# Order of the first K projection, shared input channels, LN2 on ScalarE and the order of group 1's stores in a pre-LN attention and MLP kernel

## The chip, the cores and the metric

The kernel runs on one core of a Trainium2 chip. The metric is the device time in microseconds of one execution, as a median of several runs. The engines are TensorE (PE in the profile, its weight loads PEld), VectorE (DVE), ScalarE (ACT), GpSimd (POOL) and SyncE (SP), which here issues most of the DMAs. Each engine takes its instructions in the order in which the program writes them.

## The reference

One transformer block over 2048 tokens of 576 channels, in bfloat16: local attention with 32 heads of 18 channels over 8 keys at a stride of 2, then an MLP of width 4608. A layer norm stands before the attention, and two stand one after the other before the MLP.

```python
def reference(A_x, A_wqkv, A_wo, B_x, B_w1, B_b1, B_w2, B_b2):
    def _A_ref(x, wqkv, wo):
        H = 32; Dh = D // H
        W, dil = 8, 2
        q, k, v = (x @ wqkv) in heads of Dh
        idx = pos[:, None] - (jnp.arange(W) * dil)[None, :]
        logits = jnp.einsum("bhsd,bhswd->bhsw", q, k at idx) * scale
        logits = jnp.where(idx >= 0, logits, -1e9)
        attn = _softmax(logits, axis=-1)
        o = jnp.einsum("bhsw,bhswd->bhsd", attn, v at idx)
        return o @ wo
    def _B_ref(x, w1, b1, w2, b2):
        y = _layernorm(x, axis=-1)
        h = _gelu(jnp.einsum("bsd,df->bsf", y, w1) + b1)
        return jnp.einsum("bsf,fd->bsd", h, w2) + b2
    h = x + _A_ref(_layernorm(x, axis=-1), A_wqkv, A_wo)
    return h + _B_ref(_layernorm(h, axis=-1), B_w1, B_b1, B_w2, B_b2)
```

## The kernel before

**Tiles and order.** The tokens stand in 16 tiles of 128, numbered so that a key two tokens back lies in the tile two numbers lower. The even tiles are projected first (0, 2, ... 14), then the odd ones. Attention and MLP take the tiles in groups of two, in the order 14, 12 (group 0), 10, 8 (group 1), 6, 4, 2, 0, then 15 down to 1. `A` is that order in the code, `EVEN` and `ODD` the order of projection. The order of all instructions on each engine is the order in which the program calls them; lists of calls (`after`, `between`, `hooks`, `loads`, and for the MLP `m1`, `ia`, `ib`) say what stands behind which step.

**A projection.** A contraction over 576 channels is four blocks of 128 and a rest of 64. Each matmul uses 64 rows of the array, so that two run side by side. `phase` (line 209) runs the two column halves (`g`) of an output: in the first phase half 0 takes rows 0 to 63 and half 1 rows 64 to 127 of five blocks (10 matmuls), in the second phase the rows change over for four blocks (8 matmuls). Between the two phases of one output stands a marker: `marker` (225) puts a no-operation on POOL that waits for the first phase, and the second phase waits for it. `visit` (230) runs the first phases of two or three outputs and then their second phases, each followed by its evacuation (`evac`), which is an activation on ScalarE for Q, K and V. Q, K and V take 24 visits, called 0 to 23 here, with two outputs each: visit 0 is K of tiles 0 and 2, visit 1 their V, the even tiles last until visit 11, the odd ones from 12. Visits 17 and 19 carry the output projection (`wo_duo`) of tiles 14 and 12 as a third output. PSUM has three pairs of banks in rotation for Q, K and V, and a pair "D" for other things.

**The rest of 64 channels.** For x (Q, K, V), block 4 of the transposed tile holds channels 448 to 575; half 0 uses 448 to 511 from it and takes 512 to 575 in place of them in block 3. For the attention output o, for the normalized h and for `wo` and `w1`, block 4 holds channels 512 to 575 twice, once for each half of the rows. `transpose_in` (177) makes the second copy by two more matmuls, `dma_out` (196) by a second short store into the DRAM tile `td`, from which a transposing DMA reads `oT` or `hnT`.

**Start.** Tile 0 is loaded in two halves, tile 2 in one. `ln1_first` (833) takes the mean of both tiles on ScalarE (line 840), the statistics on DVE (846, 855), and subtracts the mean on DVE (`center`, 821). `ln1_even_rstd` (857) takes the roots on POOL. `tr_x` (260) transposes both tiles on PE and copies them (267), the first on ScalarE, part of the second on DVE. Visit 0 comes after both.

**LN2 of the first two tiles.** After visit 17, `ln2` (462) adds x to the output projection of tile 14 on DVE (457) and takes statistics on DVE (148, 149, 155); behind it comes `att_qk_a` of tile 10. After visit 18 the root is taken on POOL, b2 is added into the residual (`add_b2`, 498) and a bias is made on DVE (170). Between the evacuations of visit 19, ScalarE applies the norm (174), and in visits 21 and 22 `tr_h` transposes tiles 14 and 12. Tile 12 follows two visits later in the same way. In visit 18, behind the second evacuation, stands `tr_o` of tile 12, whose copy `oT` (420) is on ScalarE. In later groups `ln2_act` (470) does the same on ScalarE: mean, square, variance (474 to 476), root on POOL (477).

**Queues.** SP's queue holds, in order, weight loads (`load`, which waits for the last evacuation), the stores and reads of K and V (`store_halo`, `halo`: a tile's ring slot is written to DRAM and read back one row lower), stores and reads of odd x (`out_x`, `in_x`: through DRAM, transposed), of o (`send_o`, `read_o`) and of normalized h, and the output stores. Wo's quarters are loaded after visits 6, 8, 11 and 12.

**Group 1 (k = 1 in the loop over groups).** In group 0's second MLP part, `read_o(e)` and an output store are issued (`ib[8]`). Group 1 begins with the weighted sum of values of tile d = 4 (`pv_sum`, with the halo load of V between its parts), its store, then QK of the next tile, the halo load of K, the read of o and seven ring stores (`halos`). The output projections of both tiles stand at the begin of its second MLP part (`ia[0]`).

Of the kernel before, what the change touches and what calls it, by code (L numbers as in the profile page):

```python
# [17 lines left out]
def kernel(  # L18
# [100 lines left out]
    def load_wo(qs):  # L119
        src = A_wo.rearrange("(h d) c -> h d c", h=H)  # L120
        for q in qs:
            load(wo_sb[q * H:(q + 1) * H, :, :], src[:, q:4 * KF:4, :])
            load(woh_sb[q * H:(q + 1) * H, :], src[:, 4 * KF + q % 2, q // 2 * HALF:(q // 2 + 1) * HALF])

    def load_w1h():
        load(b1_bf[:], B_b1.rearrange("(ft p) -> ft p", p=P))
        src = B_w1[KF * P:D, :].rearrange("p (u g c) -> p u g c", u=NU // 3, g=2)
        for r in range(2):
            load(w1h_sb[half_rows(r), :].rearrange("p (u c) -> p u c", u=NU // 3), src[:, :, r, :])

    def load_w1(c):
        cols = slice(c * F // 6, (c + 1) * F // 6)
        load(w1_sb[:, :, cols], B_w1[0:KF * P, cols].rearrange("(k p) c -> p k c", p=P))

    def load_w2(c):
        f0, f1 = (0, 4, 7, 11, 14, 21, FA, FT)[c:c + 2]
        dst = w2a_sb[:, f0:f1, :] if f1 <= FA else w2b_sb[:]
        load(dst, B_w2[f0 * P:f1 * P, :].rearrange("(ft p) c -> p ft c", p=P))
# [38 lines left out]
    def transpose_in(pair, src, twice=True):  # L177
        def turn(rows, kt, c):
            for r in range(2):
                block = src[half_rows(r), c:c + P if rows.start is None else D]  # L180
                nc.tensor.matmul(pair[rows, r, kt * HP:(kt + 1) * HP], lhsT=block, rhs=ident[half_rows(r), half_rows(r)],
                                 start=True, stop=True, skip_group_check=True)

        for kt in range(KT):
            turn(slice(None), kt, min(kt * P, D - P))
        if twice:
            turn(half_rows(0), KF, KF * P)
# [8 lines left out]
    def dma_out(src):  # L196
        td = dram.tile([P, KT * P], BF16, tag="td", name="td", bufs=4)
        nc.sync.dma_start(out=td[:, 0:D], in_=src)
        stored[0] = nc.sync.dma_start(out=td[:, D:KT * P], in_=src[:, KF * P:D]).ins
# [6 lines left out]
    def half_rows(r):  # L206
        return slice(r * HP, (r + 1) * HP)

# [21 lines left out]
    def visit(makes, hook=None, between=(), late=None):  # L230
# [6 lines left out]
        for make in makes:  # L237
# [3 lines left out]
            elif isinstance(hook, dict) and len(duos) in hook:  # L241
                hook[len(duos)]()
        for n in range(len(makes) + (late is not None)):
# [16 lines left out]
    def tr_x(j, tag):  # L260
        pair = psum_pair(tag or "CAB"[(ring_pos[0] + 1) % 3], "xt_pt")
        transpose_in(pair, q_all[:, j, :], False)
# [26 lines left out]
    def store_halo(j, ts=slice(0, 2)):  # L289
        nc.sync.dma_start(out=kv_dram[j, 1:P + 1, ts, :], in_=kv_ring[j % 2][:, j // 2, ts, :])  # L290

    def qkv_duo(j, t):
        def make():
# [3 lines left out]
            def op(g, i, sl, kt):  # L297
                c0 = g * HALF
                if g == 0 and kt == KF - 1 and sl.start:
                    kt = KF  # L300
# [126 lines left out]

    def read_o(j):
        nc.sync.dma_start_transpose(out=new_oT(j)[:], in_=o_sent.pop(j)[:])
# [3 lines left out]
    def wo_duo(j, tag):  # L433
        def make():
# [3 lines left out]
            def op(g, i, sl, kt):  # L438
                c0 = g * HALF
                return t[sl, kt, :], (wo_sb[sl, kt, c0:c0 + HALF] if kt < KF else woh_sb[sl, :])  # L440
# [29 lines left out]
    def ln2_act(j):  # L470
        h = h_of[j]
        y = sb.tile([P, D], BF16, tag="hn", name="hn", bufs=2)
        nmean, var, rstd = (sb.tile([P, 1], F32, tag=f"ln2_{t}", name=f"ln2_{t}", bufs=2) for t in ("nmean", "var", "rstd"))
        nc.scalar.activation(out=y[:], in_=h[:], func=ACT.Identity, scale=-1.0 / D, accum_out=nmean[:])
        nc.scalar.activation(out=y[:], in_=h[:], func=ACT.Square, bias=nmean[:], accum_out=var[:])
        nc.scalar.activation(out=var[:], in_=var[:], func=ACT.Identity, scale=(1.0 + EPS) / D, bias=eps2[:])
        ins = nc.gpsimd.tensor_tensor(out=rstd[:], in0=var[:], in1=mhalf[:], op=ALU.pow).ins  # L477
        root[0] = ins if j not in GROUPS[1] else None
        hn[j] = (h, rstd, nmean, y)

    def ln2_send(j):
# [3 lines left out]
        hn[j] = dma_out(y[:])  # L485
# [56 lines left out]
    def mlp1_duo(grp, us, tag):  # L542
        def make():
# [5 lines left out]
            def op(g, i, sl, kt):  # L549
                f0 = fts[g][i] * P  # L550
                c0 = (GF * us[i // GF] + i % GF) * P
                return (w1_sb[sl, kt, f0:f0 + P] if kt < KF else w1h_sb[sl, c0:c0 + P]), ht[sl, kt, 0:N]
# [225 lines left out]
    with tc.manual_schedule(engines={ENG.PE, ENG.Activation, ENG.DVE, ENG.SP, ENG.Pool}):  # L778
# [8 lines left out]
        load_wqkv(2, 0, 2)  # L787
        load_wqkv(2, 2, KF)
        load_wqkv_tail(nc.sync, 2)
        load_x(EVEN[3:4])  # L790
# [42 lines left out]
        def ln1_first():  # L833
            junk = q_all[:, ODD[-1], :]
            parts = []
            for gi in range(2):
                x = x_all[:, EVEN[gi], :]
                stats, mv, nmean = (qp.tile([P, n], F32, name=f"ln1_{gi}_{t}") for t, n in
                                    (("stats", 2 * nc.vector.BN_STATS_DIM), ("mv", nc.vector.BN_AGGR_DIM), ("nmean", 1)))
                nc.scalar.activation(out=junk, in_=x, func=ACT.Identity, scale=-1.0 / D, accum_out=nmean[:])  # L840
                parts.append((x, halves(stats[:]), mv, nmean))
                ln1[gi] = (mv[:].unsqueeze(1), None)

            def stat(gi, c):
                x, stats, _, _ = parts[gi]
                nc.vector.bn_stats(out=stats[:, c, :], in_=x[:, c * HALF:(c + 1) * HALF])

            for gi in range(2):
                stat(gi, 0)
                if gi == 0:  # L850
                    stat(gi, 1)
                center(EVEN[gi], parts[gi][3][:, 0:1], ALU.add)
                if gi == 1:
                    stat(gi, 1)
                nc.vector.bn_aggr(out=parts[gi][2][:], in_=parts[gi][1])
# [24 lines left out]
        ln1_first()  # L880

# [41 lines left out]
        for n, v in enumerate((19, 19, 20, 20, 21, 22)):  # L923
# [18 lines left out]
            17: [c_(ln2, A[0]), c_(att_qk_a, A[2])],  # L942
# [194 lines left out]
```

## Time and profile before

| what | value |
|---|---|
| median of 3 runs | 362.56 us (362.54 to 363.0) |
| the profiled execution | 366.0 us |
| its span, first to last instruction | 364.2 us |
| mean granted TensorE clock | 0.994 |
| PE busy | 355.0 us (97%), 4942 matmuls |
| DVE busy | 296.6 us (81%) |
| ACT busy | 235.3 us (65%) |
| POOL busy | 45.5 us (13%) |
| DMA | 46.29 MB, mean 127 GB/s |

The busy digits of PE and its granted clock in 40 equal slices of 9.1 us, with those of DVE between them:

```profile
PE   7999999999999799999999999999999999999996
DVE  5999999999989889994799989989998998520431
PEclk9999999999999989999999999999999999999999
```

A digit is the busy share in tenths, 9 is 90% or more; for PEclk it is the granted clock. The profile takes one execution. A wait is put down to what came last by the semaphores, so a wait for several things names one of them. Spans on POOL are rough.

### The profile page before, as it was taken

What the parts mean: (1) busy time and instruction counts of PE and PEld (TensorE: products, weight loads), DVE (VectorE), ACT (ScalarE), POOL (GpSimd) and SP (SyncE); (2) the same over time, 40 slices, a digit from 0 to 9 for tenths busy, and PEclk for the clock granted to TensorE, in tenths of its full rate; (3) what the DMA queues carried; (4) which work ended last, traced back from release to release, by engine and by line L of the source; (5) the groups of instructions that cost most, each with busy time, mean ns of one, the idle gap of its engine ahead of it and who ended that gap; (6) DMA issues with size and microseconds to landing.
All of it is one profiled execution on the core that took longest, in us unless ns stands there. A gap on an engine that the chain in (4) does not pass through costs nothing.

```text
span 364.2 us, 11562 instructions
## 1 busy us (share of the span) xinstructions
PE 355.0 (97%) x4942; PEld 292.8 (80%) x4942; DVE 296.6 (81%) x417; ACT 235.3 (65%) x521; POOL 45.5 (13%) x61
## 2 busy tenths in 40 slices
PE   7999999999999799999999999999999999999996
PEld 3778977887789777887788778877887788778874
DVE  5999999999989889994799989989998998520431
ACT  4879756897637782468846956695669566805630
POOL 2240004000112010100020102020202020210000
PEclk9999999999999989999999999999999999999999
DMA  7986799963447584651283466344545354263001
GB/s 247 329 278 191 197 218 306 373 227 72 143 90 110 174 207 71 114 90 39 74 121 81 62 133 93 90 98 122 86 88 65 93 85 58 52 120 51 4 1 32
DMA packets 62980, 46.29 MB, mean 127 GB/s; under 512 B 32192, under 2 KB 60736, under 8 KB 62928
## 3 DMA queue, kind: packets, MB, share of 16 engines
q1 hardware_dynamic: 58960, 41.50, 43.2%
q0 software_dynamic: 3744, 3.84, 9.9%
q8 instruction: 38, 0.62, 0.7%
q10 hardware_dynamic: 224, 0.22, 0.2%
q14 instruction: 14, 0.11, 0.1%
HBM read 23.38 MB, written 12.42 MB: 98 GB/s over the span
## 4 chain that ended last, share of the span: by engine, by line
PE 79%; DVE 11%; DMA 6%; ACT 2%; issue 1%; POOL 0%; ACTq 0%; SPq 0%; POOLq 0%
PE pm L216 33%; PE po L664 25%; PE po L576 9%; PE pq L216 7%; PE pw L216 4%; DVE ln_stats L148 2%; DMA x_all<-in_A_x_dram 2%; DMA oT<-td 2%; DVE prod L393 1%; DMA xnT<-xd 1%; DVE prod L399 1%; DVE prod L347 1%; ACT h_all L557 1%; DVE ln_mv L149 1%; DVE prod L338 1%
## 5 line engine op out<-in xcount | busy, mean ns | idle before, releaser
L216 PE MATMUL pm<-hnT,w_sb 64*128 64x256 bf16 x2304 | 143.0, 269 | 0.0
L557 ACT ACTIVATE h_all<-pm,b_sb 128x256 f16<-128x256 f32 (+1 forms) x288 | 108.6, 496 | 51.0 <-PE pm L216 50.4
L216 PEld LDWEIGHTS <-w_sb 64*128 64x128 bf16 x2304 | 113.5, 94 | 13.4 <-issue 1.7
L664 PEld LDWEIGHTS <-h_all 128*128 128x128 f16 x480 | 46.2, 98 | 13.7 <-issue 1.6
L216 PE MATMUL pq<-wq_sb,xnT 64*128 64x288 bf16 x720 | 54.7, 283 | 1.1 <-ACT kv_ring L306 0.4
L216 PEld LDWEIGHTS <-xnT 64*128 64x128 bf16 x864 | 44.0, 94 | 9.9 <-issue 0.8
L347 DVE TENSOR_TENSOR prod<-prod 128x2304 bf16<-128x2304 bf16 (+1 forms) x64 | 44.2, 691 | 2.0
L338 DVE TENSOR_TENSOR prod<-kv_ring,q_all 128x4608 bf16<-128x4608 bf16 x16 | 40.9, 2556 | 3.2 <-POOL ln_rstd L477 2.5
L393 DVE TENSOR_TENSOR prod<-kv_ring,probs 128x4608 bf16<-128x4608 bf16 x16 | 40.9, 2558 | 0.8 <-DMA kv_ring<-kv_dram 0.3
L216 PE MATMUL pm<-hnT,w1h_sb 64*128 64x256 bf16 x288 | 39.5, 269 | 0.0
L664 PE MATMUL po<-w2a_sb,h_all 128*128 128x288 bf16 (+1 forms) x262 | 35.8, 286 | 0.0
L576 PEld LDWEIGHTS <-h_all 128*128 128x128 bf16 x288 | 28.3, 99 | 8.7 <-issue 1.2
L399 DVE TENSOR_TENSOR prod<-prod 128x2304 bf16<-128x2304 bf16 (+1 forms) x32 | 33.9, 1058 | 1.1
L664 PEld LDWEIGHTS <-kv_ring 128*128 128x128 f16 x252 | 24.6, 98 | 6.3
L576 PE MATMUL po<-w2a_sb,h_all 128*128 128x288 bf16 x224 | 29.6, 293 | 0.0
L216 PE MATMUL pq<-wqh_sb,xnT 64*128 64x288 bf16 x144 | 27.6, 283 | 0.0
L766 POOL DMA_DIRECT2D x_all<-o_sb x12 | 10.7, 890 | 126.1 <-PE pw L216 72.2
L216 PE MATMUL pw<-wo_sb,oT 64*128 64x288 bf16 x256 | 20.1, 288 | 2.4 <-DMA oT<-td 2.3
L644 DVE TENSOR_TENSOR kv_ring<-h_all 128x1536 f16<-128x1536 f16 (+3 forms) x9 | 6.8, 760 | 16.1 <-ACT h_all L557 16.1
L664 PE MATMUL po<-w2b_sb,h_all 128*128 128x288 bf16 (+1 forms) x122 | 19.7, 286 | 0.1
L216 PEld LDWEIGHTS <-oT 64*128 64x128 bf16 x288 | 13.8, 95 | 7.0 <-DMA oT<-td 3.3
L161 POOL TENSOR_TENSOR ln_rstd<-ln_veps,mhalf 128x1 f32<-128x1 f32 (+2 forms) x14 | 13.3, 964 | 48.5 <-DVE ln_veps L155 31.7
(107 smaller groups left out, 394.9 us busy)
## 6 DMA issues: line engine op xcount, KB each, us to landing
w_sb<-in_B_w_dram SPq DMA_DIRECT2D x6, 768.0 KB, 5.8
kv_ring<-kv_dram SPq DMA_DIRECT2D x28, 144.0 KB, 2.3
kv_dram<-kv_ring SPq DMA_DIRECT2D x13, 288.0 KB, 3.9
x_all<-in_B_b_dram SPq DMA_DIRECT2D x15, 144.0 KB, 3.7
w2a_sb<-in_B_w_dram SPq DMA_DIRECT2D x2, 1008.0 KB, 7.4
td<-q_all SPq DMA_DIRECT2D x14, 144.0 KB, 1.8
td<-hn SPq DMA_DIRECT2D x14, 144.0 KB, 1.8
x_all<-h POOLq DMA_DIRECT2D x14, 144.0 KB, 4.6
```

What stands on the lines that cost most here:

```text
L148: nc.vector.bn_stats(out=stats[:, i, c, :], in_=src[:, c * HALF:(c + 1) * HALF])
L161: nc.gpsimd.tensor_tensor(out=rstd[:], in0=veps[:], in1=mhalf[:].to_broadcast([P, n]), op=ALU.pow)
L216: last = nc.tensor.matmul(duo["g"][r ^ swap][i], lhsT=lhsT, rhs=rhs, start=(swap == 0 and i == 0 and kt == 0), stop=(swap == 1 and kt == K ...
L338: ins = nc.vector.tensor_tensor(out=prod[:], in0=k_ring[j % 2], in1=q_all[:, j, :].unsqueeze(1) .to_broadcast([P, W, D]), op=ALU.mult).ins
L347: nc.vector.tensor_tensor(out=prod[:, :, o * H:o * H + n], in0=prod[:, :, a * H:a * H + n], in1=prod[:, :, c * H:c * H + n], op=ALU.add)
L393: nc.vector.tensor_tensor(out=prod[:].rearrange("p w (d h) -> p w d h", h=H), in0=v_ring[j % 2].rearrange("p w (d h) -> p w d h", h=H), in ...
L399: nc.vector.tensor_tensor(out=prod[:, 0:n, :], in0=prod[:, 0:n, :], in1=prod[:, n:2 * n, :], op=ALU.add)
L557: pace[0] = nc.scalar.activation(out=hT(grp)[:, f, 0:N], in_=ps[:, r, i * N:(i + 1) * N], func=ACT.Gelu_apprx_tanh, bias=b1_sb[:, f:f + 1] ...
L576: nc.tensor.matmul(banks[half], lhsT=hT(grp)[:, f, i * P:(i + 1) * P], rhs=w2_rows(f)[:, half * HALF:(half + 1) * HALF], start=(f == 0), s ...
L644: nc.vector.tensor_tensor(out=s_slot(t, m0, m1), in0=a, in1=b, op=alu)
L664: nc.tensor.matmul(bank, lhsT=l, rhs=r, start=start, stop=stop, skip_group_check=True)
L766: nc.gpsimd.dma_start(out=x_of(j), in_=o_of.pop(j), accum_op=ALU.add)
```

## The change

It has five parts.

1. `load_wo`, `load_w1`, `load_w1h`, `transpose_in`, `dma_out`, the operands of `wo_duo` and of `mlp1_duo`: block 4 now holds channels 448 to 575 for o, Wo, LN2 and w1 too, as it does for x. The two additional matmuls of a transpose go. The last two quarters of Wo and the sixths 0, 2 and 4 of w1 are loaded in more pieces. w2 is loaded in five pieces instead of seven.
2. Start: the first tile alone is normalized with ScalarE's mean; the second one is normalized like the later ones (`ln1_even(1)`). Its transposes stand after the first phase of the first K projection, and visit 0 runs each output's second phase and evacuation right behind its first (`apart`). The load of the fourth even tile stands before the second half of V's weights.
3. LN2 of tile 14 is on ScalarE: h on DVE and the mean on ScalarE after visit 17, square, variance and root behind the first evacuation of visit 18, the norm behind the first one of visit 19.
4. Group 1's stores: the output store of tile 14 moves from group 0's second part to group 1's last step of its first part, the halo load of V for tile d behind the store of o, and the seven ring stores wait until the read of o has landed.
5. The helper functions that these need.

```diff
     def load_wo(qs):
         src = A_wo.rearrange("(h d) c -> h d c", h=H)
         for q in qs:
-            load(wo_sb[q * H:(q + 1) * H, :, :], src[:, q:4 * KF:4, :])
-            load(woh_sb[q * H:(q + 1) * H, :], src[:, 4 * KF + q % 2, q // 2 * HALF:(q // 2 + 1) * HALF])
+            rows, k = slice(q * H, (q + 1) * H), KF - q // 2
+            load(wo_sb[rows, 0:k, :], src[:, q:4 * k:4, :])
+            if q >= 2:
+                load(wo_sb[rows, k, 0:HALF], src[:, q + 4 * k + 2, 0:HALF])
+                load(wo_sb[rows, k, HALF:D], src[:, q + 4 * k, HALF:D])
+            load(woh_sb[rows, :], src[:, 4 * KF - 2 + q, q // 2 * HALF:(q // 2 + 1) * HALF])
...
     def load_w1(c):
         cols = slice(c * F // 6, (c + 1) * F // 6)
-        load(w1_sb[:, :, cols], B_w1[0:KF * P, cols].rearrange("(k p) c -> p k c", p=P))
+        n = KF - 1 if c % 2 == 0 else KF
+        load(w1_sb[:, 0:n, cols], B_w1[0:n * P, cols].rearrange("(k p) c -> p k c", p=P))
+        for r in range(2 * (KF - n)):
+            load(w1_sb[half_rows(r), n, cols], B_w1[n * P + 2 * r * HP:n * P + 2 * r * HP + HP, cols])
 
     def load_w2(c):
-        f0, f1 = (0, 4, 7, 11, 14, 21, FA, FT)[c:c + 2]
+        f0, f1 = (0, 7, 14, 21, FA, FT)[c:c + 2]
...
-    def transpose_in(pair, src, twice=True):
...
-        if twice:
-            turn(half_rows(0), KF, KF * P)
+    def transpose_in(pair, src):
+        for kt in range(KT):
+            c = min(kt * P, D - P)
             for r in range(2):
...
     def dma_out(src):
         td = dram.tile([P, KT * P], BF16, tag="td", name="td", bufs=4)
-        nc.sync.dma_start(out=td[:, 0:D], in_=src)
-        stored[0] = nc.sync.dma_start(out=td[:, D:KT * P], in_=src[:, KF * P:D]).ins
+        nc.sync.dma_start(out=td[:, 0:KF * P], in_=src[:, 0:KF * P])
+        stored[0] = nc.sync.dma_start(out=td[:, KF * P:KT * P], in_=src[:, D - P:D]).ins
...
+    def block(g, sl, kt):
+        return KF if g == 0 and sl.start and kt == KF - 1 else kt
...
     def visit(makes, hook=None, between=(), late=None, apart=False):
...
+            if apart:
+                phase(duos[-1], 1, marks[-1])
+                duos[-1]["evac"]()
+        if apart:
+            return
...
     def read_o(j):
-        nc.sync.dma_start_transpose(out=new_oT(j)[:], in_=o_sent.pop(j)[:])
+        o_read[0] = nc.sync.dma_start_transpose(out=new_oT(j)[:], in_=o_sent.pop(j)[:]).ins
...
-                return t[sl, kt, :], (wo_sb[sl, kt, c0:c0 + HALF] if kt < KF else woh_sb[sl, :])
+                return t[sl, block(g, sl, kt), :], (wo_sb[sl, kt, c0:c0 + HALF] if kt < KF else woh_sb[sl, :])
...
     def ln2_act(j):
+        ln2_mean(j)
+        ln2_root(j)
+
+    def ln2_mean(j):
...
         nc.scalar.activation(out=y[:], in_=h[:], func=ACT.Identity, scale=-1.0 / D, accum_out=nmean[:])
+        hn[j] = (h, rstd, nmean, y, var)
+
+    def ln2_root(j):
+        h, rstd, nmean, y, var = hn[j]
         nc.scalar.activation(out=y[:], in_=h[:], func=ACT.Square, bias=nmean[:], accum_out=var[:])
         nc.scalar.activation(out=var[:], in_=var[:], func=ACT.Identity, scale=(1.0 + EPS) / D, bias=eps2[:])
         ins = nc.gpsimd.tensor_tensor(out=rstd[:], in0=var[:], in1=mhalf[:], op=ALU.pow).ins
-        root[0] = ins if j not in GROUPS[1] else None
+        root[0] = ins if j not in GROUPS[0] + GROUPS[1] else None
...
-    def ln2_send(j):
+    def ln2_norm(j):
         h, rstd, nmean, y = hn[j]
         nc.scalar.activation(out=nmean[:], in_=nmean[:], func=ACT.Identity, scale=rstd[:])
         ln_apply_act(y[:], h[:], rstd[:], nmean[:])
-        hn[j] = dma_out(y[:])
+        hn[j] = y
...
         load_wqkv(2, 0, 2)
+        load_x(EVEN[3:4])
         load_wqkv(2, 2, KF)
         load_wqkv_tail(nc.sync, 2)
-        load_x(EVEN[3:4])
...
         ln1_first()
+        ln1_even(1)
...
-        for n, v in enumerate((19, 19, 20, 20, 21, 22)):
+        for n, v in enumerate((19, 20, 21, 22)):
...
-            17: [c_(ln2, A[0]), c_(att_qk_a, A[2])],
-            18: [c_(ln2_rstd, A[0]), c_(add_b2, A[0]), c_(ln2_bias, A[0]), c_(halo, A[2], 1), c_(att_qk_add, A[2], ((0, 0, 9),))],
+            17: [c_(ln2_h, A[0]), c_(ln2_mean, A[0]), c_(att_qk_a, A[2])],
+            18: [c_(add_b2, A[0]), c_(halo, A[2], 1), c_(att_qk_add, A[2], ((0, 0, 9),))],
...
-            18: {1: [c_(tr_o, A[1], "D")]},
-            19: [c_(ln2_hn, A[0])],
+            18: {0: [c_(ln2_root, A[0])], 1: [c_(tr_o, A[1], "D")]},
+            19: [c_(ln2_norm, A[0])],
...
         hooks = {
+            0: {1: lambda: call([c_(tr_x, EVEN[1], "C"), c_(ln1_even, 2)])},
...
-        tr_x(EVEN[1], "C")
-        ln1_even(2)
...
-            visit(duos, hooks.get(qd), between.get(qd, ()))
+            visit(duos, hooks.get(qd), between.get(qd, ()), apart=qd == 0)
...
         def halos(n):
             for _ in range(min(n, len(pending_halo))):
-                store_halo(pending_halo.pop(0))
+                ins = store_halo(pending_halo.pop(0))
+                if o_read[0] is not None:
+                    tc.add_manual_dep(ins, o_read[0].name, sync_dep, reason="stores behind the read of o")
...
-                ib[8] = [c_(read_o, e), c_(out_store, g[0])]
+                ib[8] = [c_(read_o, e)]
             elif k == 1:
-                m1[0] += [c_(pv_sum, d), c_(send_o, d)]
+                m1[0] += [c_(att_pv_sum, d), c_(send_o, d), c_(halo, d, 2)]
                 m1[1] += [c_(att_qk_a, e), c_(halo, e, 1), c_(read_o, d), c_(att_qk_b, e, 0), c_(halos, 7)]
-                m1[3] += [c_(att_qk_a, f), c_(halo, f, 1), c_(att_qk_add, f, ((0, 0, 9), (0, 0, 4)))]
+                m1[3] += [c_(out_store, GROUPS[0][0]), c_(att_qk_a, f), c_(halo, f, 1), c_(att_qk_add, f, ((0, 0, 9), (0, 0, 4)))]
```

## The prediction

> **What bounds the kernel now.** I read four views, in this order. The table of waits by engine comes first, because TensorE (PE) is busy 355.0 of 364.2 us and only its idle time can be won. The lines give who waited for whom, the total, the number of waits and the longest one.
>
> ```profile
> PE pw L216 <- DMA oT<-td: 2.3, 2, 2.2
> PE xt_pt L181 <- DVE q_all L821: 1.4, 2, 1.2
> PE pq L216 <- ACT kv_ring L306: 0.4, 2, 0.2
> PE pq L216 <- POOLq L226: 0.2, 1, 0.2
> ```
>
> Two waits matter: the output projection that waits for an attention tile (2.2 us once), and the start, where the second tile's transposes wait for its centring (1.2 us). Then the timeline of PE and of SP's queue around the first (start, us, engine, line, operation, count, idle time before it):
>
> ```profile
> 124.34 0.30 PE L216 MATMUL pw<-woh_sb,oT 64*128 64x288 bf16 x2
> 126.80 0.66 PE L216 MATMUL pw<-wo_sb,oT 64*128 64x288 bf16 x8 [2.15 <-DMA oT<-td]
> 129.00 8.15 PE L576 MATMUL po<-w2a_sb,h_all 128*128 128x288 bf16 x56
> 138.95 7.02 PE L576 MATMUL po<-w2a_sb,h_all 128*128 128x288 bf16 x56
> ...
> 116.27 0.58 SPq L769 DMA_DIRECT2D out_dram<-x_all  x1
> 116.90 0.43 SPq L333 DMA_DIRECT2D kv_ring<-kv_dram  x1
> 117.87 0.45 SPq L199 DMA_DIRECT2D td<-q_all  x1
> 122.19 1.21 SPq L429 DMA_TRANSPOSE oT<-td  x1
> 123.45 4.80 SPq L290 DMA_DIRECT2D kv_dram<-kv_ring  x7
> ```
>
> The reader should see that the same 56 matmuls take 8.15 us after the wait and 7.02 us later, and that the tile's store (117.87) stands behind an output store and a halo load, while its read (122.19) shares the DMA engines with seven ring stores. The third view, stretches of one us, tells why the matmuls are slow (stretch, length, PE busy and count, granted clock, DMA share, GB/s):
>
> ```profile
> 129.00:130.00 1.00, 1.00 (x7) 0.50 1.04 396
> 132.00:133.00 1.00, 1.00 (x11) 1.00 1.06 80
> ```
>
> The granted clock is 0.50 here. The same stretches put the drop at about 127.9 to 131.3: 3.4 us at half speed, so 1.7 us lost on top of the 2.15. The fourth view is the order on the engines where LN2 moves, visits 18 and 19, with ScalarE's own price for the same work taken from group 1:
>
> ```profile
> 52.72 0.75 DVE L457 TENSOR_TENSOR h<-pw,x_all 128x576 f32<-128x576 f32 x1
> 53.16 1.19 ACT L306 ACTIVATE kv_ring<-pq 128x576 bf16<-128x576 f32 x2 [1.82 <-PE pq L216]
> 54.24 0.70 ACT L420 CAST oT<-o_pt 128x640 bf16<-128x640 f32 x1
> 56.52 0.65 ACT L306 ACTIVATE q_all<-pq 128x576 bf16<-128x576 f32 x1 [1.58 <-issue]
> ...
> 128.94 0.68 ACT L474 ACTIVATE hn<-h 128x576 bf16<-128x576 f32 x1 [2.13 <-DVE h L457]
> 129.75 0.77 ACT L475 ACTIVATE hn<-h,ln_nmean 128x576 bf16<-128x576 f32 x1
> 130.65 0.29 ACT L476 ACTIVATE ln_var<-ln_var,eps 128x1 f32<-128x1 f32 x1
> 130.85 0.67 ACT L474 ACTIVATE hn<-h 128x576 bf16<-128x576 f32 x1
> ```
>
> Start to start, the mean costs 0.81 us, the square 0.90 and the variance 0.20.
>
> **Start.** The second tile loses ScalarE's mean (5.27 to 6.05), so the first tile's copies can start at about 5.47 instead of 5.96 (transposes end 5.36, plus 0.12 as at 10.43 to 10.55). The first K projection then runs from 5.9, held by its weights (second half landed at 6.18, tail about 0.4 later) to about 6.7. DVE now takes both statistics before the second centring, which ends at about 6.68 instead of 6.45; the second transposes follow at 6.75, and its DVE copy still starts at about 7.16 (7.17 before), ScalarE's copy behind it. So the second projection starts at 7.64 as before, and only 0.24 us comes out of the visit: the eight matmuls of the first tile's second phase (8.53 to 9.02, 0.49) now lie ahead of it, but the marker between the second tile's phases has no cover any more (its first phase issues until 8.53, its last matmul ends at 8.69, POOL answers at 8.73 to 8.75), which costs 0.25. The third change is larger: tile 6's load (the fourth even tile) waits at 5.21 for a DMA slot and holds DVE for 0.62 us at 9.57. Issued at 3.97 in place of a weight half it lands near 8.25, and DVE runs 0.66 earlier; PE, which waits for centrings in visits 1 to 3, follows. I count 0 of this. At 51.23 PE already waits (0.15) for xnT, whose read is issued at 46.09 once a store has landed; the time won before ends there. Bounds: -0.7 to 0.
>
> **Shared channels.** Eight 64-column matmuls go (two in each of four transposes). Ten of them issue in 0.13 us, so 0.1 us is won. Matmul counts of projections and MLP stay. The stores of a turned tile keep their two DMAs and 160 KB. Wo's last two quarters and w1's even sixths become four and three DMAs: 4 + 6 more issues, two fewer for w2. SP issues one in 0.44 us (44.57 to 45.01). For w1 SP is idle before and after and nothing waits. For Wo, four issues (1.75 us) stand ahead of the xnT read at 46.09, two of them ahead of the halo load at 44.10. With DVE 0.66 early SP begins 0.66 sooner, so the halo load leaves at about 44.1 as before, and the xnT read at 46.4 to 46.6. Visit 18 starts 0.4 late (bounds -0.7 to +1).
>
> **LN2 on ScalarE.** DVE sheds 0.82 + 0.21 + 0.15 + 0.15 us, but its next step, adding b2, waits for b2's load (landed 57.47), so nothing is won there. ScalarE runs in order: the mean waits for h, which ends at 53.47, and behind it stand both evacuations of visit 18 and the copy of the next o. My clock for ScalarE: mean 53.5 to 54.3, evacuation to 54.9 (0.55 apart), square to 55.75, variance to 55.95, evacuation to 56.55, copy of o (0.70) to 57.2, against 54.94 before. Visit 19's output projection, which used oT at 55.16, starts at 57.25. What is left of the visit then is 34 matmuls of 0.061 (18 pairs in 1.1 us), 2.07 us, so it ends at 59.3, not 57.24. Visit 20 has 36 of them, 2.2 us, and visit 21 starts at 61.5 instead of 59.81. There part of an old wait covers the rest: its second phase stood until 61.66 for the marker behind the other tile's root, and now comes at 61.5 + 1.22 + 0.13 = 62.9. Net **+1.25 us** with visit 18's 0.4 in it. If h comes 0.66 earlier it is +0.5; if the halo load is a us late, +2.1. The root on POOL took 2.80 us beside a QK product at 54.84 and 0.56 at 131.10; at 56 DVE idles for b2, so it is short, and the markers queued behind it are not yet due.
>
> **Group 1's stores.** The output store and the halo load leave the queue ahead of the o stores: these go at about 116.3 and 116.7, 1.2 us sooner, and wait less (before, 4.3 us to land; the median of such stores is 1.8). The read follows at about 121 and, with the seven ring stores held until it has landed, should take nearer its median of 2.9 than the 4.56 of before: 124. PE comes there at 124.65 + 1.25 - 0.1 = 125.8. So the wait of 2.15 goes and the clock drop with it, 1.7. What SP holds back are the ring stores, from 123.45 to 124, and behind them output stores, b2 and LN2's store, which waits for ScalarE until 133.95 anyway. Later nothing takes it back: the transposed LN2 tiles land at 141.4 for 147.87, and DVE waits 5.00 us for PE at 169.16.
>
> The Trainium skill (TensorE: Matmul & The Clock Gate, HAM oscillation) asks for no PE gaps above some 3.4 us. By that rule a gap of 2.15 us drops no clock; the trace shows a drop after just this gap, and I follow the trace. By the rule the sum would be 1.7 us smaller.
>
> **Sum**, against the profiled execution's own 366.0 us (span 364.2): -0.1 + 1.25 - 2.15 - 1.7 = **-2.7 us**. The median of the plain runs, 362.56, lies 3.4 below the profiled one, and I can't see which idle time is shorter there. With the same change: **359.9 us**, own range 358.9 to 361.2.
>
> **Rivals.**
> 1. *The wait goes, but no clock drop is won*: it is not in the plain runs, or the 1.7 us idle in visit 19 brings another one. For it: 0.50 is granted for one 3.4 us stretch only, and 1.2 us of idle at the start brought no drop. Sum -1.0: 361.5 us.
> 2. *The read of o still comes late*, landing at 127 (issued 122.2, 4.6 us). PE then waits about 1 us and the clock may hold: -1.6, 361.0 us. Against it: two DMAs fewer ahead and no ring stores beside it.
> 3. *ScalarE's queue decides, slower*: the stall of visit 19 (1.15 net of the transposes, up to 2.0) stays, while the wait at 126.80 is an effect of the profiled execution's slower DMAs and absent in plain runs. The 3.4 us by which these are shorter is close to 2.15 + 1.7, which speaks for it; that the queue's order needs no profiler to be late speaks against. 363.7 us; it decides once the wait and its drop cost under 1.15 us in plain runs.
>
> **Chances.** Forecast 0.51, rival 1 0.22, rival 2 0.07, rival 3 0.20. A plain measurement tells 0.2% (0.73 us) from no change. The forecast gives faster nearly always, rival 1 in six of ten cases, rival 2 mostly; rival 3 slower in seven of ten, else same. Faster 0.67, same 0.16, slower 0.17. The range runs from 358.9 to 363.6, to leave out part of rival 3.
>
> **What would show it.** Right: no PE wait for oT in group 1, granted clock 1.0 through 127 to 132, the 56 matmuls at 7.0 us, and a new PE wait for ScalarE's oT or kv_ring of 1.5 to 2 us near 55 to 57. Wrong: a clock drop near 56 to 60, PE waiting over 0.5 us for oT near 126, or xnT reads that hold visit 18 by over 1 us.

## The result, and the profile after

| | before | after |
|---|---|---|
| median | 362.62 us (362.48 to 363.0) | 364.73 us (364.25 to 365.8) |
| ratio, 95% interval | 1 | 1.0065 [1.0051, 1.0078] |
| profiled execution, its span | 366.0, 364.2 us | 364.67, 362.9 us |

The change makes the kernel slower by 0.65%, some 2.4 us. The forecast was faster, 359.9 us, and its range ended at 363.6.

The profiled executions alone say the opposite: 364.67 after 366.0. So the first thing to settle is which of the two profiles is like the plain runs. The one of after is (364.67 beside a median of 364.73); the one of before lies 3.4 us above its median. Before unchanged was therefore profiled again, as the first experiment (span 361.1 us, 362.85 in all), and its lines are used below as "the second profile of before". Of the 110 plain executions of before that were recorded beside the experiments, 16 show a mean clock of 0.994 or 0.995, like the first profile (0.994): twelve of these took 361.05 to 363.85 us, as the others did (361.03 to 364.87), and four 365.7 to 368.17.

The table of waits of the kernel after answers to the first view of before (who waited for whom, total, number, longest):

```profile
PE pm L221 <- DMA hnT<-td: 1.5, 2, 1.3
PE pq L221 <- DMA xnT<-xd: 1.3, 1, 1.3
PE pw L221 <- ACT oT L429: 1.1, 1, 1.1
...
PE pw L221 <- DMA oT<-td: 0.4, 1, 0.4
```

The two waits of before, for oT's read in group 1 and for the second centring at the start, are gone. Three others are the largest now: for a transposed LN2 tile, for a transposed x tile, and for ScalarE's copy of o.

The timeline of the kernel after in group 1, TensorE first and then SP's queue (start, us, engine, line, operation, count):

```profile
123.64 2.80 PE L221 MATMUL pm<-hnT,w_sb 64*128 64x256 bf16 x48
126.27 0.67 PE L221 MATMUL pw<-wo_sb,oT 64*128 64x288 bf16 x8
...
128.58 7.03 PE L599 MATMUL po<-w2a_sb,h_all 128*128 128x288 bf16 x56
...
117.02 0.83 SPq L200 DMA_DIRECT2D td<-q_all  x1
117.89 0.45 SPq L201 DMA_DIRECT2D td<-q_all  x1
118.39 1.55 SPq L342 DMA_DIRECT2D kv_ring<-kv_dram  x2
120.92 1.24 SPq L440 DMA_TRANSPOSE oT<-td  x1
123.81 1.29 SPq L300 DMA_DIRECT2D kv_dram<-kv_ring  x3
```

Here the picture is the predicted one: the read leaves at 120.92, the ring stores stand behind it, the output projection follows without idle time, and the 56 matmuls take 7.03 us. The one-us stretches of the same place (stretch, length, PE busy, its weight loads, DVE, ACT and POOL with counts, granted clock, DMA share, GB/s) agree:

```profile
129.00:130.00 1.00, 1.00 (x11) 0.80 (x9) 0.97 (x3) 0.97 (x4) 0.00 (x0) 1.00 0.96 356
132.00:133.00 1.00, 1.00 (x10) 0.78 (x8) 0.96 (x3) 0.97 (x4) 0.00 (x0) 1.00 0.70 75
```

The clock is 1.00 in both. And yet the same output projection, used for the second tile, starts no earlier than in before: 127.37 here, 127.30 in the first profile of before, where it had waited 2.15 us. What after saves here beside the first profile, it had lost before. The timeline of visits 18 to 20 in the kernel after shows where (TensorE, then ScalarE, then DVE; in brackets the idle time before, and what ended it):

```profile
52.06 0.66 PE L221 MATMUL pq<-wq_sb,xnT 64*128 64x288 bf16 x8 [1.29 <-DMA xnT<-xd]
...
56.90 0.66 PE L221 MATMUL pw<-wo_sb,oT 64*128 64x288 bf16 x8 [1.08 <-ACT oT L429]
...
53.29 0.68 ACT L489 ACTIVATE hn<-h 128x576 bf16<-128x576 f32 x1 [2.25 <-DVE h L468]
...
53.99 0.65 ACT L315 ACTIVATE kv_ring<-pq 128x576 bf16<-128x576 f32 x1
54.54 0.77 ACT L494 ACTIVATE hn<-h,ln_nmean 128x576 bf16<-128x576 f32 x1
...
56.16 0.68 ACT L429 CAST oT<-o_pt 128x640 bf16<-128x640 f32 x1
...
58.93 0.76 DVE L522 TENSOR_TENSOR x_all<-h,x_all 128x576 bf16<-128x576 f32 x1 [3.21 <-DMA x_all<-in_B_b_dram]
...
60.87 0.75 DVE L468 TENSOR_TENSOR h<-pw,x_all 128x576 f32<-128x576 f32 x1
```

Visit 18 stands 1.29 us for the read of x, visit 19 stands 1.08 us for the copy of o behind LN2 on ScalarE, and DVE stands 3.21 us for b2. The last is the largest and the least visible (before: 0.27 us in the first profile, 0.77 in the second): DVE is not the busiest engine, but its next step, h of tile 12 at 60.87, leads into a chain of attention steps without much idle time that ends in the output projection of group 0's second tile (92.74) and, through LN2 and its transposing read, in the start of group 1's MLP (108.58, with the wait of 1.26 for hnT).

SP's queue in the kernel after says why b2 is late:

```profile
45.15 1.31 SPq L104 DMA_DIRECT2D wo_sb<-in_A_wo_dram  x3
46.52 0.41 SPq L104 DMA_DIRECT2D woh_sb<-in_A_wo_dram  x1
47.03 1.33 SPq L290 DMA_TRANSPOSE xnT<-xd  x1
48.47 0.53 SPq L286 DMA_DIRECT2D xd<-q_all  x1
...
52.76 1.85 SPq L290 DMA_TRANSPOSE xnT<-xd  x1
54.71 0.52 SPq L104 DMA_DIRECT2D x_all<-in_B_b_dram  x1
```

A quarter of Wo takes four issues instead of two, the read behind it leaves at 47.03, the store of the next odd x behind that, the read of this x waits for its store (52.76), and the load of b2 stands behind this read (54.71, landed at 58.8).

### The profile page after: what moved, and what is told of

Its sections match the earlier page's. It is cut to its first block, busy times and chain, and to the rows that moved or that the text cites. A ratio compares the mean times of both kernels' runs of the same rounds, so it can differ in the third digit from the quotient of the medians.

```text
span 362.9 us, 11553 instructions
## 1 busy us (share of the span) xinstructions
PE 353.3 (97%) x4934; PEld 295.6 (81%) x4934; DVE 295.2 (81%) x412; ACT 236.2 (65%) x525; POOL 44.1 (12%) x61
## 4 chain that ended last, share of the span: by engine, by line
PE 72%; DVE 13%; DMA 7%; ACT 3%; SPq 2%; issue 2%; POOL 0%; POOLq 0%; ACTq 0%
PE pm L221 34%; PE po L687 22%; PE pq L221 7%; PE po L599 5%; PE pw L221 4%; DVE ln_stats L155 2%; DVE prod L356 2%; DMA hnT<-td 2%; DMA x_all<-in_A_x_dram 1%; DVE prod L402 1%; DMA td<-hn 1%; DVE prod L347 1%; DVE prod L408 1%; DMA xd<-q_all 1%; ACT h_all L580 1%
## 5 line engine op out<-in xcount | busy, mean ns | idle before, releaser
L221 PEld LDWEIGHTS <-w_sb 64*128 64x128 bf16 x2304 | 115.2, 94 | 13.3 <-issue 2.9
L221 PE MATMUL pq<-wq_sb,xnT 64*128 64x288 bf16 x720 | 55.8, 288 | 2.4 <-DMA xnT<-xd 1.3
L221 PEld LDWEIGHTS <-xnT 64*128 64x128 bf16 x864 | 45.0, 95 | 11.2 <-DMA xnT<-xd 1.9
L599 PE MATMUL po<-w2a_sb,h_all 128*128 128x288 bf16 x224 | 28.5, 286 | 0.0
L496 POOL TENSOR_TENSOR ln_rstd<-ln_var,mhalf 128x1 f32<-128x1 f32 x14 | 9.8, 697 | 108.3 <-ACT ln_var L495 108.3
```

Source lines behind the costliest of these rows:

```text
L221: last = nc.tensor.matmul(duo["g"][r ^ swap][i], lhsT=lhsT, rhs=rhs, start=(swap == 0 and i == 0 and kt == 0), stop=(swap == 1 and kt == K ...
L599: nc.tensor.matmul(banks[half], lhsT=hT(grp)[:, f, i * P:(i + 1) * P], rhs=w2_rows(f)[:, half * HALF:(half + 1) * HALF], start=(f == 0), s ...
```

## The experiments

Each kernel was timed in five rounds beside before on one chip. The theory at the outset was: the wait and the clock drop of group 1 belong to one execution (rival 3's condition), and the loss comes from LN2's order on ScalarE, from the added Wo pieces in SP's queue, or from both. All ratios are to before on the same chip. The table stands in four groups of four kernels, each group on a chip of its own; the medians of before beside them are 363.03, 362.18, 361.86 and 362.93 us. So medians compare only within a group, and times from traces of different chips with a margin of about 1 us.

| kernel | median, us | ratio, 95% interval |
|---|---|---|
| before again | 363.46 | 1.0016 [0.9990, 1.0041] |
| before + channels | 366.39 | 1.0099 [1.0059, 1.0139] |
| before + LN2 | 363.79 | 1.0021 [0.9997, 1.0044] |
| before + stores | 363.45 | 1.0006 [0.9984, 1.0029] |
| before + start | 361.31 | 0.9990 [0.9970, 1.0009] |
| after, Wo's last quarters early | 366.03 | 1.0098 [1.0063, 1.0132] |
| after, LN2 on DVE | 364.76 | 1.0083 [1.0067, 1.0099] |
| after without channels | 362.41 | 1.0014 [1.0002, 1.0027] |
| after, b2 early | 363.77 | 1.0061 [1.0036, 1.0086] |
| after, Wo's quarters whole | 363.65 | 1.0055 [1.0035, 1.0075] |
| after, w1's sixths whole | 364.21 | 1.0054 [1.0035, 1.0072] |
| before + start + stores + b2 early | 361.21 | 0.9980 [0.9968, 0.9991] |
| after again | 364.34 | 1.0054 [1.0034, 1.0075] |
| after, Wo whole + b2 early | 363.32 | 1.0018 [1.0001, 1.0035] |
| the same, LN2 re-ordered | 362.36 | 1.0001 [0.9985, 1.0018] |
| without channels, b2 early, LN2 re-ordered | 361.25 | 0.9962 [0.9949, 0.9975] |

**Before again.**

> The kernel before, unchanged, for a second trace of it. If the profiled execution of before was an unusual one, this one shows a span near 360.8 us (362.6 less 1.8), no clock drop at 128 us and a wait for oT in group 1 under 0.6 us. If the wait belongs to the kernel, it shows 2 us of wait again and a span near 364. Time: same, ratio 1.000.

The waits and the timeline of this second profile of before:

```profile
PE pw L216 <- DMA oT<-td: 0.2, 1, 0.2
```

```profile
122.04 2.80 PE L216 MATMUL pm<-hnT,w_sb 64*128 64x256 bf16 x48
124.66 0.67 PE L216 MATMUL pw<-wo_sb,oT 64*128 64x288 bf16 x8
...
126.98 7.03 PE L576 MATMUL po<-w2a_sb,h_all 128*128 128x288 bf16 x56
...
58.30 0.76 DVE L499 TENSOR_TENSOR x_all<-h,x_all 128x576 bf16<-128x576 f32 x1 [0.77 <-DMA x_all<-in_B_b_dram]
...
60.31 0.75 DVE L457 TENSOR_TENSOR h<-pw,x_all 128x576 f32<-128x576 f32 x1
...
45.08 0.42 SPq L104 DMA_DIRECT2D woh_sb<-in_A_wo_dram  x1
46.15 1.32 SPq L280 DMA_TRANSPOSE xnT<-xd  x1
...
54.23 0.50 SPq L104 DMA_DIRECT2D x_all<-in_B_b_dram  x1
...
121.64 1.21 SPq L429 DMA_TRANSPOSE oT<-td  x1
122.91 5.27 SPq L290 DMA_DIRECT2D kv_dram<-kv_ring  x7
```

No wait for oT of more than 0.2 us, no pause before the 56 matmuls, and these take 7.03 us: the stall and the clock drop (3.85 us together) belong to the execution that was profiled first, not to the usual run of the kernel. The order of the queue is the same in both profiles: here, too, seven ring stores leave right behind the read of o (122.91 and 121.64). But the read lands after 2.8 us, where it took 4.6 in the first profile; why it took longer there isn't shown. Against this profile the kernel after comes 1.6 us later at the second tile's output projection (127.37 against 125.77) and at group 1's MLP (108.58 against 106.98). Of this, 0.5 us stand at the output projection of group 0's second tile already (92.74 against 92.25); most of the rest is the wait for hnT, 1.26 us against 0.15.

**The four parts alone on before**: the channels with w2's five pieces; LN2 of tile 14 on ScalarE; group 1's stores; the new order at the start with the earlier load.

> Before, with the shared channels alone (Wo and w1 in more pieces, w2 in fewer). Queue theory: SP issues four more Wo pieces ahead of the read of xnT, b2's load follows later by 1 to 1.5 us, DVE waits for b2 longer (0.3 to over 1 us) and its chain up to group 0's MLP is late by as much: slower by 1.0 to 2.0 us, 363.6 to 364.6. ScalarE theory (LN2's order is the cause): within 0.4 us of before.

> Before, with LN2 of tile 14 on ScalarE alone. ScalarE theory: PE waits 1 to 2 us for oT's copy in visit 19 and the end comes 1 to 2 us later, 363.6 to 364.6. Queue theory: PE waits there too, but DVE's chain sets group 0's MLP and doesn't move, so the wait is made up: within 0.5 us of before, 362.3 to 363.1.

> Before, with the order of group 1's stores alone. If the wait and the drop belong to before's plain runs: 2 to 3.8 us faster, 359 to 360.5. If they were in one execution only: within 0.7 us of before, 361.9 to 362.7, and no wait for oT in group 1.

> Before, with the start alone (order of the first K projection and the earlier load of the fourth even tile). Both theories: DVE's chain of the first norms runs up to 0.7 us earlier, and what PE wins is lost at the read of xnT unless SP's queue comes earlier too: 361.9 to 362.6, -0.7 to 0. If the clock is still at half speed in visit 0, up to 1 us slower.

The channels cost about 1%, more than the whole change and more than the 1 to 2 us expected. LN2 costs about 0.2%, but its interval still holds no change; the stores bring nothing that can be measured (the read of o lands after 2.8 us, as in the second profile of before), the start at most 0.3%. The timeline of before with the channels, SP's queue and then DVE:

```profile
47.77 0.41 SPq L104 DMA_DIRECT2D woh_sb<-in_A_wo_dram  x1
48.29 1.33 SPq L290 DMA_TRANSPOSE xnT<-xd  x1
...
55.93 0.52 SPq L104 DMA_DIRECT2D x_all<-in_B_b_dram  x1
...
60.06 0.76 DVE L522 TENSOR_TENSOR x_all<-h,x_all 128x576 bf16<-128x576 f32 x1 [1.94 <-DMA x_all<-in_B_b_dram]
```

The read leaves 2.14 us later than in the second profile of before (48.29 against 46.15); 0.77 of this is there before the first of these Wo loads (43.18 against 42.41), so about 1.4 is left for the four added issues. It lands 3.8 later (5.3 us after its issue, where it took 3.6; in the first profile of before, without the pieces, it took 5.1), and visit 18 starts 2.3 later (53.63 against 51.37). The addition of b2 is 1.76 us later (60.06 against 58.30), the output projection of group 0's second tile 1.88 (94.13 against 92.25), group 1's MLP 2.3 (109.29 against 106.98). The two profiled times differ by 3.2 us (366.04 and 362.85): the last 0.9 arises between 169 and 204 us, at a wait for hnT (0.36) and one for oT (0.26) among others, and was not followed further.

**Parts taken out of after.**

```diff
-        for q, v in enumerate((6, 8, 11, 12)):
-            loads[v] = [c_(load_wo, [q])]
+        for q, v in enumerate((6, 8, 4, 5)):
+            loads[v] = loads.get(v, []) + [c_(load_wo, [q])]
```

> The changed kernel, with the last two quarters of Wo (four pieces each) loaded after visits 4 and 5, when SP's queue is idle, instead of 11 and 12. Queue theory: the reads of xnT and the load of b2 come 1 to 1.5 us earlier, DVE's chain with them, and the kernel gains 1.2 to 2.4 us: 362.3 to 363.5. ScalarE theory: gains under 0.5 us, 364.2 or more.

A miss: 1.0098. The queue is no freer after visits 4 and 5. There the pieces stand ahead of the first odd x tiles' stores, whose read leaves at 34.76 instead of 30.95; visit 12 starts 2.1 us later (38.18 against 36.10), and the read at 47.03 comes later too (48.12). The block was moved, not taken away.

```diff
-            17: [c_(ln2_h, A[0]), c_(ln2_mean, A[0]), c_(att_qk_a, A[2])],
-            18: [c_(add_b2, A[0]), ...
+            17: [c_(ln2, A[0]), c_(att_qk_a, A[2])],
+            18: [c_(ln2_rstd, A[0]), c_(add_b2, A[0]), c_(ln2_bias, A[0]), ...
```

> The changed kernel with LN2 of tile 14 on DVE as before. ScalarE theory: the PE wait of 1.1 us in visit 19 goes and 1 to 2 us are won: 362.7 to 363.7. Queue theory: within 0.5 us of the changed kernel, 364.2 to 365.2, or slower still, since DVE gets 1.3 us of statistics back, partly inside its wait for b2.

Taking LN2 back brings nothing in after (1.0083, beside 1.0065 and 1.0054 for after itself). In its trace the wait for ScalarE's oT is gone, while the addition of b2 stands at 59.52 and h of tile 12 at 61.53: DVE's chain, not the stall, sets what follows. Alone on before the same stall (1.4 us) went with some 0.2%, not clear of nothing.

> The changed kernel without the shared channels (start, LN2 and stores stay). Queue theory: nothing stands ahead of xnT's read and b2's load: 362.0 to 362.9, like before or a little faster. ScalarE theory: 364 or more, since LN2's order is still there.

Without the channels 1.0014: about half a per cent comes back, with the stall of visit 19 still there (1.4 us). The add of b2 starts at 56.48 and h of tile 12 at 58.42, against 58.93 and 60.87:

```profile
56.48 0.76 DVE L520 TENSOR_TENSOR x_all<-h,x_all 128x576 bf16<-128x576 f32 x1 [1.51 <-DMA x_all<-in_B_b_dram]
...
58.42 0.75 DVE L466 TENSOR_TENSOR h<-pw,x_all 128x576 f32<-128x576 f32 x1
```

This trace is 0.76 us ahead of that of after already at the first of these Wo loads (41.20 against 41.96), so by estimate some 1.7 of the 2.45 us are the queue's. At the output projection of group 0's second tile 1.27 us are left (91.47 against 92.74), for there TensorE sets the pace: from 60 to 108 us the chain that ended last holds TensorE alone, while in after DVE's steps are the largest part of it.

**The queue cut at two places.** b2's load one step earlier, or Wo's quarters in whole pieces. The latter leaves out the four extra pieces, so that block 3 of two quarters holds other rows; the w1 kernel leaves out six pieces in the same way.

```diff
-            13: [c_(ln1_act, 10, 1), c_(in_x, 2), c_(out_x, 3)],
-            14: [c_(att_pv, A[1]), c_(in_x, 3), c_(load, b2_bc, B_b2.partition_broadcast(P))],
+            13: [c_(ln1_act, 10, 1), c_(in_x, 2), c_(out_x, 3), c_(load, b2_bc, B_b2.partition_broadcast(P))],
+            14: [c_(att_pv, A[1]), c_(in_x, 3)],
```

> The changed kernel, with b2's load one visit earlier in SP's queue (behind the last store of odd x instead of behind the last read of xnT). Queue theory with b2 as the link: b2 lands by 54, DVE adds it as soon as its QK product ends (55.7), its chain comes 1.3 to 1.5 us earlier from there to group 0's MLP, and the kernel gains 1.2 to 1.6 us against the changed one: ratio to before about 1.003 instead of 1.0065 to 1.008. If the late read of xnT itself is the link (PE's 1.3 us of wait), nothing is won: ratio 1.0065 or more.

> The changed kernel with each quarter of Wo loaded in two DMAs as before; it leaves out the four extra pieces, so the last block of two quarters holds other rows of Wo. Queue theory: the read of xnT is issued 1 to 1.7 us earlier, b2 lands 1 to 1.4 us earlier, and 1 to 1.5 us are won: ratio 1.003 to 1.005. If w1's pieces or the new layout are the cause, the ratio stays at 1.0065 to 1.008.

> The changed kernel with each sixth of w1 loaded in one DMA as before; it leaves out the six extra pieces, so one block of w1 holds other rows. Queue theory: w1's pieces stand at idle places of SP's queue or behind b2: within 0.4 us of the changed kernel, ratio 1.006 to 1.009. If w1's pieces are the cause: ratio 1.002 to 1.005.

None of the three alone can be told from after, by its ratios of 1.0065 and 1.0054 (it was not run beside them). The traces suggest why for the first two. With b2 early, DVE adds it at 55.91, but visit 18 still waits 1.9 us for xnT and visit 19 1.1 us for oT, so h of tile 12 (59.68) now waits for TensorE. With Wo whole the wait for xnT is gone, but b2 still lands at 58.0 and h comes at 60.11. Each cut leaves the other link. If so, both have to be cut together.

> Before, with the start and the stores of the change and b2's load one visit earlier; no shared channels, LN2 on DVE. Queue theory with b2 as the link: 1 us from the start (DVE's chain 0.7 to 1.5 earlier) and 0.5 to 1 us from b2, so 360.5 to 361.3 where before has 362.5: ratio 0.994 to 0.997. If b2 isn't the link: like the start alone, ratio 0.998 to 1.000.

This one measures 0.9980, like the start alone and not as expected of b2 as the link. DVE adds b2 without a wait there, but only at 57.24: in this kernel, without the channels and with LN2 on DVE, b2's load holds nothing up that could be measured.

> The changed kernel unchanged, beside the next three on one chip. Ratio to before 1.0065 again (1.005 to 1.008), and in the trace a wait for xnT of 1 us and more in visit 18 and b2 landing after 58 us.

> The changed kernel with Wo in whole quarters (two quarters' last block holds other rows) and b2's load one visit earlier: both links of the queue theory cut at once. If they are two bounds of nearly the same length, cutting both gives more than either alone (0.1% each): 1.2 to 2 us won, ratio 1.001 to 1.003, with the wait for ScalarE's oT of 1 to 1.4 us as the last one left in visits 18 to 21. If the queue is not the cause, ratio 1.005 or more.

Together they bring after from 1.0054 [1.0034, 1.0075] to 1.0018 [1.0001, 1.0035], on one chip; the intervals just meet. In the traces the output projection of group 0's second tile moves from 92.74 to 91.55 and group 1's MLP from 107.98 to 106.65. What is left in the waits of this kernel, and DVE's timeline in it:

```profile
PE pw L218 <- ACT oT L426: 1.4, 1, 1.4
```

```profile
55.26 0.75 DVE L519 TENSOR_TENSOR x_all<-h,x_all 128x576 bf16<-128x576 f32 x1
55.93 1.35 DVE L353 TENSOR_TENSOR prod<-prod 128x2304 bf16<-128x2304 bf16 x1
58.78 0.76 DVE L465 TENSOR_TENSOR h<-pw,x_all 128x576 f32<-128x576 f32 x1 [1.50 <-PE pw L218]
```

DVE no longer waits for b2; it waits 1.50 us for the output projection, and this for ScalarE. So the stall that cost nothing in after sets the start of this step here. The next kernel puts mean, square and variance behind both evacuations and the copy of o, and the root behind visit 19's markers on POOL:

```diff
-            17: [c_(ln2_h, A[0]), c_(ln2_mean, A[0]), c_(att_qk_a, A[2])],
+            17: [c_(ln2_h, A[0]), c_(att_qk_a, A[2])],
...
-            18: {0: [c_(ln2_root, A[0])], 1: [c_(tr_o, A[1], "D")]},
-            19: [c_(ln2_norm, A[0])],
+            18: {1: [c_(tr_o, A[1], "D"), c_(ln2_mean, A[0]), c_(ln2_root, A[0])]},
+            19: [c_(ln2_pow, A[0]), c_(ln2_norm, A[0])],
```

> As the last, with LN2 of tile 14 still on ScalarE, but its mean, square and variance behind both evacuations and the copy of oT in visit 18, and its root on POOL behind visit 19's markers. ScalarE's order costs PE 1 to 1.4 us in visit 19 there: that wait goes, and DVE keeps the 1.3 us it shed: a further 0.7 to 1.4 us, ratio 0.997 to 1.000. If the order costs nothing at the end: like the last one, within 0.3 us.

> Start, stores, LN2 on ScalarE in the order of the last one, b2's load one visit earlier, no shared channels: nothing of the queue's and of ScalarE's cost is left. 359.8 to 360.9 where before has 362: ratio 0.994 to 0.997. If the shared channels were worth keeping, it is no faster than the last one.

With the new order the wait for ScalarE's oT is gone, h of tile 12 starts at 57.44 instead of 58.78, and the median is 0.96 us lower; the intervals overlap, so the size is not sure. The last kernel drops the channels and keeps everything else: **0.9962 [0.9949, 0.9975]**, 361.25 us, faster than both kernels of this study. The b2 load and the order on ScalarE, which the change doesn't have, belong to it.

From the last but one to the last kernel the channels (without the extra pieces of Wo, which the last but one leaves out) cost another 0.4%, some 1.4 us, though none of the links above is left. Their traces part late: the output projection of group 0's second tile at 90.76 and 90.59, group 1's MLP at 105.88 and 105.11. So 0.6 us arise in between; where the rest arises was not found. In between stands the store of LN2's second tile. SP's queue with the channels, and then without:

```profile
97.84 0.38 SPq L197 DMA_DIRECT2D td<-hn  x1
98.27 0.42 SPq L198 DMA_DIRECT2D td<-hn  x1
101.62 2.53 SPq L518 DMA_TRANSPOSE hnT<-td  x2
```

```profile
97.79 1.07 SPq L198 DMA_DIRECT2D td<-hn  x1
98.92 0.42 SPq L199 DMA_DIRECT2D td<-hn  x1
100.59 2.53 SPq L519 DMA_TRANSPOSE hnT<-td  x2
```

In both kernels the first store begins at 97.8; the read, which leaves when both stores have landed, leaves at 101.62 or 100.59. This holds in all traces: in the ten with shared channels (128 KB and 32 KB stored) the first of these two stores lands after 2.8 to 3.5 us and the read leaves 10.8 to 11.4 us after the output projection; in the eight without (144 KB and 16 KB) it is 2.4 to 2.7 us and 10.0 to 10.6 us. The median of the larger stores of LN2 is 1.7 to 1.8 us in both forms. Why this one does is open: the layout of the store, the DMAs around it, or their turn in the queue were not told apart.

## Why the prediction was wrong

**"Sum against the profiled execution": the terms -2.15 and -1.7.** This is the step that turned the sign: it counted as a gain a wait and a drop of an execution that lies 3.4 us above the median. Both are gone in after, as listed under "Right", but that is not the change's doing: the second profile of before has 0.2 us of that wait and a clock of 1.0, and the stores alone give 1.0006 [0.9984, 1.0029]. Nor do these runs show the reason given for the slow read, the output store ahead and the ring stores beside it: in the old order (second profile) and in the new one (stores alone) it lands after 2.8 us alike. The warning was in the working itself: the median lay 3.4 us below the profiled time, "and I can't see which idle time is shorter there". The two terms come to 3.85 us. Without them the sum is +1.15 us, where some 2.4 were measured. Rival 3 named this condition, at 0.20, and its 363.7 us is the nearest, but the price it went by, ScalarE's stall, isn't what the runs show: the channels are.

**"Visit 18 starts 0.4 late (bounds -0.7 to +1)".** Within its bounds against the profile that it was read from, where visit 18 starts at 51.23 (52.06 in after, 0.83 late), but twice the size, and the lead that the start gives (0.96 us at this visit, alone on before) hides more. Beside the kernel without channels visit 18 starts 1.9 late (52.06 against 50.17), some 1.1 without the lead of that trace at the Wo loads. A sign that the working had listed under "Wrong" came: the read holds visit 18 by 1.29 us.

**"Its next step, adding b2, waits for b2's load (landed 57.47), so nothing is won there."** The wait is there, but the question stopped at it. b2's load stands in the same queue as the Wo pieces, behind two reads of x and the store between them, and DVE's chain after it leads to group 1. In after b2 lands at 58.8, against 56.4 without channels. The term that was missing is the price of a later b2 and a later read of x together: with both cut, group 0's second output projection comes 1.2 us earlier, and the kernel gains 0.36% (from 1.0054 to 1.0018). No rival had it.

**LN2 on ScalarE, +1.25 with visit 18's 0.4 in it.** The order came as worked out: copy of o done at 56.84 (predicted 57.2), output projection at 56.90 (57.25), stall 1.08 us (the prediction's 1.7); 1.4 where visit 18 isn't late. Alone it measures +0.2%, 0.8 us, close to the 0.85 that is left without the 0.4; but the interval holds nothing, and in the trace group 1's MLP starts only 0.24 later than in the second profile of before (107.22 against 106.98), so the agreement may be luck. In after the same stall is covered by DVE's wait for b2.

**Start, 0 (-0.7 to 0).** Alone 0.9990 [0.9970, 1.0009], about -0.4 us, inside the bounds. But "the time won before ends there" did not hold: with the start alone visit 18 begins 0.96 us earlier (50.41 against 51.37), since the read ahead of it leaves earlier too (45.40 against 46.15).

**Shared channels, -0.1 for the transposes; "for w1 SP is idle before and after and nothing waits".** w1 whole doesn't differ from after, as predicted. The small gain of the transposes could not be seen beside the rest. The other cost of the channels wasn't foreseen: the working took the stores as unchanged ("keep their two DMAs and 160 KB"), and the one at 98 to 102 lands later; 0.6 us arise there between the last two kernels.

**The clock.** The forecast followed the trace where the Trainium skill (TensorE: Matmul & The Clock Gate, HAM oscillation) names a gap of some 3.4 us. Idle times of 1.3 us (after), 1.7 us (Wo early) and 1.9 us (b2 early) in visit 18 brought no drop in these runs. The single drop among the matmuls followed the single gap of 2.15 us. A clock of 0.50 also stands behind the last matmul of several traces: in "after, Wo whole + b2 early" the last one ends at 357.6, and the clock drops at 359.9, after 2.3 us without a matmul. So a drop after a gap below 3.4 us is not a single case, but no run puts a gap of 2 us among matmuls to the test again. The point doesn't decide the sign, since the gap itself was absent.

The sum of the parts as they measure alone is +1.0 + 0.2 + 0.1 - 0.1 = 1.2%, about twice the change's 0.65%: that LN2's stall and b2's wait lie beside each other instead of one behind the other explains a part at most, since the channels alone cost 1.0% on before (interval 0.6 to 1.4%) and about 0.4 to 0.5% in after. The rest stays open.

## What to carry to other kernels

Before a stall is counted as a gain, see whether the profiled time agrees with the plain runs; where it is longer by about the size of the stall, take a second profile, and until then work the sum without the stall. When a DMA is pushed back in an in-order queue, follow every later transfer of this queue to who waits for it, not only the next one: a part of the cost here arose several transfers further back, on an engine that the change had relieved. Two links that end at nearly the same time can show no gain when either is cut alone, so a null result for one of them doesn't clear it.

## What was not expected of the hardware

Most issues of a plain DMA on SP took 0.35 to 0.55 us in the lines above, but single ones took 1.2 to 1.4 us (in after the first Wo load at 41.96 took 1.23, the w1 load at 49.91 took 1.40); what held these isn't shown. And the one store of LN2 that lands after 2.8 us or more in all ten traces with the 128 + 32 KB form, and after 2.7 us or less in all eight with 144 + 16 KB, stores the same 160 KB in two DMAs in both.
